# An FNet + SoLU kernel: three parts of the first transform turned later and by GpSimd, and the mean of the first four steps on ScalarE

## Chip, cores, metric

One core of one Trainium2 chip. The metric is the device time in microseconds (us), with the median of several executions. Profiles show one execution; times in them count from its start. "Faster" or "slower" needs 2%.

Names used throughout: PE is the matrix engine, DVE is VectorE, ACT is ScalarE, POOL is GpSimd, SP is SyncE. A "q" after the name of an engine is its sequencer. PEld is PE's loading of weights, which overlaps with its products (from 96 to 1140 us of the kernel before, PE is busy for all 1044 us and PEld for 797 of them).

## The reference

All is float32.

```python
x = randn(8, 3136, 256) * 0.1                       # batch, sequence, features
X = np.fft.fft(np.fft.fft(x, axis=1), axis=2).real  # FNet mixing
x = X.reshape(25088, 256)
h = x @ w_in                                        # 256 -> 1024
solu = h * softmax(h)
ln = (solu - mean) / sqrt(var + 1e-6) * g_ln
out = ln @ w_out                                    # 1024 -> 256
```

## The kernel before

The transform along the sequence (3136 = 49 x 64) is done in two stages. The result of the first stage goes to DRAM (`zd`). It is then read back with its axes changed, in five parts for each pair of batches: that is "turning" a part. Each part takes four requests of 160 KB:

```python
def turn(pr, i, engine=nc.gpsimd, a=0, b=KG):
    zd = pr.zd.rearrange("(k j) n d -> j n k d", j=4)
    ...
    for j in range(4):
        engine.dma_start(out=pr.g[i][j * NH : (j + 1) * NH, a:b, :], in_=zd[j, :, i * KG + a : i * KG + b, :])
```

The second stage and the expert layer then run in 100 steps, one `Unit` each. In each step PE computes `up` of the present unit, `transform2` for the unit two steps ahead, and `down` of the unit four steps back. A unit needs one row `r` of 512 bytes, spread by a DMA of its own (`spread`), before DVE can make `ev`. The operations that the change touches, and the loop:

```python
def spread(t):                                   # the tiny transfer "r"
    t.r = small.tile([P, 1], FP32, tag="r", name="r")
    nc.sync.dma_start(out=t.r, in_=t.q[0:1, P : 2 * P])

def product(t, s):                               # u = h * exp, with its sum; then -mean
    ...
    nc.vector.scalar_tensor_tensor(out=t.u[s], in0=t.h[s], scalar=1.0, in1=t.u[s], op0=ALU.mult,
                                   op1=ALU.mult, accum_out=t.usum[:, s : s + 1])
    nc.gpsimd.tensor_scalar(out=t.nmean[:, s : s + 1], in0=t.usum[:, s : s + 1], scalar1=-1.0 / FF,
                            scalar2=None, op0=ALU.mult)

def square(t, s):                                # (u - mean)^2, summed, on ScalarE
    ...

whole = 4                                        # these steps transpose u on PE, later ones by DVE and DMA
for i in range(len(units) + lag):                # lag = 4
    ...
        even(cur, up(cur, 0))                    # ev: waits for r
        ...
        ps_o = [down(old, s) for s in order]
        ...
        for s in cur.signs:
            product(cur, s)
        if i == 1:
            weights.centre()                     # wbar, then DVE centres the output weights
        for s in cur.signs:
            square(cur, s)
        ...
    if 0 < i + 1 < NK // KG:
        turn(first, i + 1, nc.sync)              # parts 1 to 4 in steps 0 to 3
    if ahd:
        ahead(ahd, cur.k1)                       # in step 0 it loads two blocks of the next pair
```

## Time and profile before

| | before | where it is read |
|---|---|---|
| time, median of 3 (range) | 1195.55 us (1193.29 to 1196.69) | the timed runs |
| span of the profiled run | 1191.5 us | page |
| PE busy | 97% | page, part 1 |
| first product of `down` starts | 96.16 us | timeline of PE |
| row r of step 3: requested, `ev` starts | 72.62, 85.52 us | chain of waits |
| last product of PE to the end of the span | 7.30 us | trace; the prediction did not look at it |

The kernel is bound by PE, which is full from 96 to 1140 us.

### The profile page before, as it was taken

What the parts mean: (1) busy time and instruction counts of PE and PEld (TensorE: products, weight loads), DVE (VectorE), ACT (ScalarE), POOL (GpSimd) and SP (SyncE); (2) the same over time, 40 slices, a digit from 0 to 9 for tenths busy, and PEclk for the clock granted to TensorE, in tenths of its full rate; (3) what the DMA queues carried; (4) which work ended last, traced back from release to release, by engine and by line L of the source; (5) the groups of instructions that cost most, each with busy time, mean ns of one, the idle gap of its engine ahead of it and who ended that gap; (6) DMA issues with size and microseconds to landing.
All of it is one profiled execution on the core that took longest, in us unless ns stands there. A gap on an engine that the chain in (4) does not pass through costs nothing.

```text
span 1191.5 us, 15914 instructions
## 1 busy us (share of the span) xinstructions
PE 1152.2 (97%) x4720; PEld 874.4 (73%) x4720; DVE 904.8 (76%) x1234; ACT 678.5 (57%) x1404; POOL 489.1 (41%) x950
## 2 busy tenths in 40 slices
PE   2979999999999999999999999999999999999997
PEld 1547777777777777778777777777777777777786
DVE  7889777777778877777768878777777887777770
ACT  4567565656546655555646656556565555565551
POOL 3034535434545444443544444442543333433342
PEclk9899999999999999999999999999999999999999
DMA  9693765756775765655775775663684444535433
GB/s 241 200 218 75 174 159 155 205 144 147 186 167 158 190 178 140 179 142 137 172 182 144 193 177 144 173 173 109 167 198 112 129 133 120 141 94 141 124 104 101
DMA packets 459797, 185.38 MB, mean 156 GB/s; under 512 B 425750, under 2 KB 442270, under 8 KB 459712
## 3 DMA queue, kind: packets, MB, share of 16 engines
q1 hardware_dynamic: 446720, 148.18, 49.3%
q0 software_dynamic: 12992, 36.19, 10.9%
q8 instruction: 38, 0.62, 0.2%
q14 instruction: 47, 0.39, 0.1%
HBM read 44.78 MB, written 38.80 MB: 70 GB/s over the span
## 4 chain that ended last, share of the span: by engine, by line
PE 93%; DMA 3%; DVE 1%; SPq 1%; issue 0%; ACT 0%; POOL 0%; DVEq 0%; ACTq 0%
PE ps_o L328 57%; PE ps_h L227 27%; PE ps L171 5%; PE ps L199 3%; DMA raw_in<-in_moe_w_in_dram 1%; DMA r<-q 1%; PE wps L459 1%; SPq L179 1%; DMA T<-in_t_tab_dram 0%; DVE y L123 0%; DVE xa L131 0%; DVE y L122 0%; ACT h L268 0%; SPq L364 0%; DVE ev L233 0%
## 5 line engine op out<-in xcount | busy, mean ns | idle before, releaser
L328 PE MATMUL ps_o<-Wo,uT 128*128 128x256 f32 x3136 | 693.2, 379 | 0.0
L328 PEld LDWEIGHTS ps_o<-Wo,uT 128*128 128x128 f32 x3136 | 611.0, 196 | 62.1 <-issue 0.9
L227 PE MATMUL ps_h<-Wi,q 128*128 128x512 f32 x800 | 361.6, 595 | 2.6 <-DVE ev L233 2.1
L259 DVE SCALAR_TENSOR_TENSOR u<-h,u 128x1024 f32<-128x1024 f32 x196 | 239.9, 1225 | 55.2 <-ACT u L251 28.8
L261 POOL TENSOR_SCALAR nmean<-usum 128x1 f32<-128x1 f32 x196 | 83.3, 425 | 455.2 <-DVE u L259 455.1
L241 DVE CUSTOM_DVE_ANT_0 h<-ev,ps_h 128x1024 f32<-128x1024 f32 x196 | 231.7, 1218 | 49.9 <-PE ps_h L227 38.6
L227 PEld LDWEIGHTS ps_h<-Wi,q 128*128 128x128 f32 x800 | 152.1, 191 | 152.2 <-issue 143.3
L268 ACT ACTIVATE h<-u,nmean 128x1024 f32<-128x1024 f32 x196 | 225.0, 1149 | 65.0 <-POOL nmean L261 64.0
L233 DVE SCALAR_TENSOR_TENSOR ev<-w_mid,r,ps_h 128x1024 f32<-128x1024 f32 x100 | 127.8, 1278 | 136.7 <-PE ps_h L227 122.5
L251 ACT ACTIVATE u<-h,neg 128x1024 f32<-128x1024 f32 x196 | 225.3, 1150 | 6.3
L296 DVE STREAM_TRANSPOSE v<-u 128x1024 f32<-128x1024 f32 x192 | 228.6, 1233 | 0.1
L205 ACT COPY q<-ps 128x256 f32<-128x256 f32 x100 | 37.0, 371 | 280.7 <-PE ps L199 245.2
L333 ACT ACTIVATE ot<-ps_o,rs 128x256 f32<-128x256 f32 x196 | 87.0, 461 | 60.2 <-PE ps_o L328 51.2
L340 POOL DMA_INDIRECT out_dram<-ot,idx x96 | 103.1, 1074 | 36.8 <-issue 20.9
L199 PEld LDWEIGHTS ps<-T,g 128*128 128x128 f32 x400 | 60.1, 191 | 48.3 <-issue 45.8
L171 PE MATMUL ps<-y,F 98*100 98x258 f32 (+3 forms) x288 | 71.4, 385 | 23.7 <-DVE y L124 23.7
L283 POOL TENSOR_TENSOR rs<-v,neg_half 128x2 f32<-128x2 f32 (+1 forms) x100 | 84.1, 841 | 7.8
L249 ACT ACTIVATE neg<-nmax 128x1 f32<-128x1 f32 x196 | 38.2, 195 | 64.8 <-DVE nmax L241 64.8
L171 PEld LDWEIGHTS ps<-y,F 98*100 98x100 f32 x288 | 45.6, 177 | 35.6 <-DVE y L124 21.6
L280 POOL TENSOR_SCALAR v<-ssq 128x2 f32<-128x2 f32 (+1 forms) x100 | 23.1, 231 | 113.9 <-ACT h L268 113.9
L199 PE MATMUL ps<-T,g 128*128 128x128 f32 x400 | 60.7, 275 | 0.6 <-DMA g<-zd 0.6
L131 POOL TENSOR_TENSOR xa<-xa,xb 98x1020 f32<-98x1020 f32 (+1 forms) x24 | 54.5, 2272 | 0.0
(72 smaller groups left out, 441.9 us busy)
## 6 DMA issues: line engine op xcount, KB each, us to landing
uT<-v SPq DMA_DIRECT2D x752, 128.0 KB
out_dram<-ot SPq DMA_DIRECT2D x100, 128.0 KB
xa<-in_x_dram SPq DMA_DIRECT2D x28, 392.0 KB
zd<-z SPq DMA_DIRECT2D x24, 400.0 KB
g<-zd POOLq DMA_DIRECT2D x60, 160.0 KB, 4.7
g<-zd SPq DMA_DIRECT2D x16, 160.0 KB
raw_in<-in_moe_w_in_dram SPq DMA_DIRECT2D x4, 512.0 KB
raw_out<-in_moe_w_out_dram SPq DMA_DIRECT2D x2, 1024.0 KB
```

Of the source, the lines that this page charges most:

```text
L171: nc.tensor.matmul(o[..., cs], F[:, 2 * t + h, :], i[..., cs], start=first, stop=True, skip_group_check=True)
L199: nc.tensor.matmul(o, g[:, k, h * P : (h + 1) * P], table, start=(h == 0), stop=True, skip_group_check=True)
L227: nc.tensor.matmul(ps[:, fs], t.q[:, c * P : (c + 1) * P], Wi[:, c, fs], start=True, stop=True)
L233: nc.vector.scalar_tensor_tensor(out=t.ev, in0=w_mid, scalar=t.r, in1=ps, op0=ALU.mult, op1=ALU.add)
L241: nc.vector.tensor_tensor_reduce(out=t.h[s], in0=t.ev, in1=ps, scale=1.0, scalar=-3.0e38, op0=ALU.subtract if s else ALU.add, op1=ALU.max, ...
L251: nc.scalar.activation(out=t.u[s], in_=t.h[s], func=ACT.Exp, bias=t.neg[:, s : s + 1], accum_out=t.esum[:, s : s + 1])
L259: nc.vector.scalar_tensor_tensor(out=t.u[s], in0=t.h[s], scalar=1.0, in1=t.u[s], op0=ALU.mult, op1=ALU.mult, accum_out=t.usum[:, s : s + 1])
L268: nc.scalar.activation(out=t.h[s], in_=t.u[s], func=ACT.Square, bias=t.nmean[:, s : s + 1], accum_out=t.ssq[:, s : s + 1])
L296: nc.vector.transpose(out=t.batch.v[:, t.w, :, o], in_=t.u[s])
L328: nc.tensor.matmul(ps, uT[:, c, :, s], Wo[:, c, :], start=(c == 0), stop=(c == KF - 1))
L333: nc.scalar.mul(out=t.ot[s], in_=ps, mul=t.rs[:, s : s + 1])
L340: dma = nc.gpsimd.indirect_dma_start(out=out, out_offset=bass.IndirectOffsetOnAxis(ap=idx[:, i : i + 1], axis=0), in_=t.ot[s], in_offset=None)
```

## The change

Two intentions. The 1.92 MB of parts 2 to 4 leave the crowded start, where SyncE's queue also carries the rows `r`, and are requested by GpSimd in steps 5, 8 and 11, shortly before they are used. And in the first four steps, the mean is made on ScalarE, so that the square, also on ScalarE, need not wait for GpSimd.

```diff
-    def product(t, s):
+    def product(t, s, alone):
...
-        nc.gpsimd.tensor_scalar(out=t.nmean[:, s : s + 1], in0=t.usum[:, s : s + 1], scalar1=-1.0 / FF,
-                                scalar2=None, op0=ALU.mult)
+        if alone:
+            nc.scalar.mul(out=t.nmean[:, s : s + 1], in_=t.usum[:, s : s + 1], mul=-1.0 / FF)
+        else:
+            nc.gpsimd.tensor_scalar(...)                      # as before
...
-                    product(cur, s)
+                    product(cur, s, i < whole)
...
-            if 0 < i + 1 < NK // KG:
-                turn(first, i + 1, nc.sync)
+            if i == 0:
+                turn(first, 1, nc.sync)
+            elif i in (5, 8, 11):
+                turn(first, (i + 1) // 3)                     # by GpSimd
```

More of the change, by code (lines that the diff above doesn't have):

```diff
@@ L260, in product @@
                                        op1=ALU.mult, accum_out=t.usum[:, s : s + 1])
-        nc.gpsimd.tensor_scalar(out=t.nmean[:, s : s + 1], in0=t.usum[:, s : s + 1], scalar1=-1.0 / FF,
-                                scalar2=None, op0=ALU.mult)
+        if alone:
+            nc.scalar.mul(out=t.nmean[:, s : s + 1], in_=t.usum[:, s : s + 1], mul=-1.0 / FF)
+        else:
+            nc.gpsimd.tensor_scalar(out=t.nmean[:, s : s + 1], in0=t.usum[:, s : s + 1], scalar1=-1.0 / FF,
+                                    scalar2=None, op0=ALU.mult)
     def square(t, s):
```

## The prediction

> **What bounds the kernel now.** I read the page first (busy times, slices, chain), then a table of windows, then the chain of the start alone, then the timelines of each engine between 58 and 130 us. Page, parts 1 and 2:
>
> ```profile
> PE 1152.2 (97%) x4720; PEld 874.4 (73%) x4720; DVE 904.8 (76%) x1234; ACT 678.5 (57%) x1404; POOL 489.1 (41%) x950
> ...
> PE   2979999999999999999999999999999999999997
> ```
>
> PE is full in every slice but those at the start and the very end. The windows (length, then busy us of PE, PEld, DVE, ACT, POOL) put the border at 96 us:
>
> ```profile
> 0.00:96.00 96.00, 63.99 (x235) 38.80 (x236) 77.06 (x138) 52.66 (x95) 25.37 (x47) 0.93 0.83 212
> 96.00:1140.00 1044.00, 1044.00 (x4291) 797.38 (x4290) 812.76 (x1077) 610.31 (x1279) 446.78 (x876) 1.00 0.59 153
> ```
>
> From 96 to 1140 us PE has no gap at all. So the change can shorten the kernel only by making that full stretch begin earlier, and lengthen it only by delaying that begin or tearing a gap into it. The first product of the down projection starts at 96.16 us. What sets that is in the chain of waits between 66 and 97 us (start, length, what):
>
> ```profile
> 66.73 5.83 DMA T<-in_t_tab_dram
> ...
> 72.62 12.80 DMA r<-q
> ...
> 85.52 1.29 DVE ev L233
> ...
> 91.77 1.15 POOL nmean L261
> ...
> 92.94 0.23 ACT h L268
> ...
> 95.32 0.26 ACT q L205
> 95.63 0.66 PE ps_t L308 x4
> ```
>
> One tiny transfer, the row r of the unit of step 3 (512 bytes, "r3" from here), holds 12.8 of these 30 us. It was requested at 72.62 and landed at 85.42. After it comes a serial chain of VectorE and ScalarE work, 10.1 us, to the last transposes of that step. The chain crosses both things that the change touches: the mean (GpSimd) and the queue in which the parts are turned (SyncE). The SyncE queue, in order:
>
> ```profile
> 65.46 2.45 SPq L445 DMA_DIRECT2D T<-in_t_tab_dram  x2
> ...
> 69.55 1.79 SPq L187 DMA_DIRECT2D g<-zd  x4
> 71.39 0.86 SPq L109 DMA_DIRECT2D xa<-in_x_dram  x2
> 72.62 0.51 SPq L210 DMA_DIRECT2D r<-q  x1
> 73.56 4.50 SPq L187 DMA_DIRECT2D g<-zd  x4
> 80.29 0.48 SPq L210 DMA_DIRECT2D r<-q  x1
> 82.47 4.25 SPq L187 DMA_DIRECT2D g<-zd  x4
> ```
>
> The reader is to see that r3 stands *ahead* of the third part (73.56) and behind the second part (69.55) and two loads of the next pair (71.39). The change takes out the groups at 73.56, 82.47 and the later one at 87.34, all behind r3. It leaves everything ahead of r3.
>
> [...] What stands behind r3 in the same queue should then not hold it up. The trace agrees. In its packet records the 196 packets of 4096 bytes of the two loads start between 76.5 and 83.7 us on the hardware queue, and r3 lands 1.4 us after the last of them. [...] from 79.5 to 81.5 us 12 to 15 packets of the loads and about 2 of the next part (1024 bytes) are open at a time. [...]
>
> **The mean, part by part.** Step 3 in the timeline of all engines:
>
> ```profile
> 85.52 1.28 DVE L233 SCALAR_TENSOR_TENSOR ev<-w_mid,r,ps_h 128x1024 f32<-128x1024 f32 x1 [4.26 <-DMA r<-q]
> ...
> 89.62 0.19 ACT L249 ACTIVATE neg<-nmax 128x1 f32<-128x1 f32 x1
> ...
> 91.60 1.22 DVE L259 SCALAR_TENSOR_TENSOR u<-h,u 128x1024 f32<-128x1024 f32 x1
> 91.77 1.35 POOL L261 TENSOR_SCALAR nmean<-usum 128x1 f32<-128x1 f32 x2 [6.63 <-DVE u L259]
> ...
> 92.94 1.15 ACT L268 ACTIVATE h<-u,nmean 128x1024 f32<-128x1024 f32 x1 [1.86 <-POOL nmean L261]
> ```
>
> The first of the two means starts at 91.77 and its row of the trace is 1.14 us long, against 0.23 for one that runs free. It sits behind the second product (91.60 to 92.82)[...]. The square starts at 92.94, 0.12 us after the second product ends. So ScalarE waits 1.86 us for a mean whose own work is 0.2 us. That looks like a gain of about 1 us, but not in the order in which the code issues: the loop makes product and mean of both signs first, then both squares. On ScalarE[...] the queue is then mean 0, mean 1, square 0, square 1. Mean 1 needs the second product, which ends at 92.82. It starts about 0.06 us later and holds ScalarE about 0.23 us (the small negation of the same shape: 0.19 long, next one 0.23 after its start). Square 0 can start at about 93.11 in place of 92.94: 0.17 us *later*. [...] On the path that adds +0.17 us in step 3. The same happens in step 2, and in step 0, which has one sign, the mean gains about 0.1 us; neither is on the path, as r3 comes later than both. In step 1 the scaling of wbar on ScalarE (0.36 us) now falls behind two means, and VectorE's centring of the output weights starts some 0.75 us later, at 72.5. VectorE idles 4.26 us before r3 lands, so this is swallowed too.
>
> **The parts turned later.** Removed from the early SyncE queue: 3 x 4 requests, 1.92 MB. Effect on r3's request: none, it waits for the table T (landed 72.55), because a request waits for the one eight earlier in that queue and T is eight before r3 in both kernels. Effect on r3's landing: the third part ran[...] until about 82 us, then beside the last 23 or so packets of the loads. Those that started at 82.1 to 82.7 took 500 to 640 ns against 290 to 370 just before. If the third part's traffic caused that, two packets in a row on the slowest engine could each save 0.25 us; if not, nothing. I take -0.2 us on the path. The next row (requested 80.29) goes out some 4.5 us earlier, but its user was not waiting for it. Added later: 4 requests on GpSimd at the end of steps 5, 8 and 11. The trace has such groups already, for the later pairs:
>
> ```profile
> 300.01 2.37 POOL L187 DMA_DIRECT2D g<-zd  x4
> ```
>
> 2.4 us each in a step of 11.65 us, in which GpSimd at that stage is busy about half (5 us in 12), and before its next mean it had 2.9 us of idle in the steps 4 and 5. A mean that comes late by a few tenths delays ScalarE, which is not the bound and feeds a product four steps on. The third part, requested near 113 us, must have landed when step 8 takes it, near 137 us; such groups landed in 4.6 us in the middle. PE stayed full through the stretches in which the later pairs do this. Cost: 0.
>
> **Sum.** +0.17 - 0.2 + 0 = about 0 us. Predicted: 1195.4 us.
>
> **Rivals.** (A) The third part does hold r3 up[...]. Then r3 would land before VectorE is through with step 2 (about 82 us), and the start would move by up to 85.5 - 82.0 = 3.5 us: 1192 us. For it: r3 takes 12.8 us, DMA share is at 1.0 throughout. Against: [...]the loads that end just before it, and that about 1.42 MB of the second part and the loads, plus the gathered rows of the GpSimd queue (0.78 MB), stand ahead and alone fill most of that time at 190 GB/s (2.2 MB: 11.6 us). (B) [...] the squares of step 3 start 1 us earlier, 1194.4 us. Against: the issue order above. (C) GpSimd's added requests in steps 5 to 11 push means and load gathers so far that PE runs dry: each gap of PE would add 1 to 3 us, 1197 to 1201 us. Against: later pairs. (D) Without the turned parts around 84 to 92 us nothing changes in PE's clock, which dips to half at 88 us[...]; it comes back by itself and those matmuls are not on the chain.
>
> **Range and chances.** The three runs before span 3.4 us by themselves, more than any of my terms. With rival A or B on one side and C on the other: 1191.5 to 1198.0 us. A change of 2% is 24 us; the whole idle time of PE between 60 and 96 us is only 7.8 us, so faster by over 2% is all but excluded (0.01), slower would need many gaps in the full stretch (0.01), the same 0.98.
>
> **What would show it.** Right: the chain of the start still has r3 landing near 85 us, the square of step 3 starts 0.25 to 0.3 us after the second product with the mean of the second sign on ScalarE ahead of it, the first down product at 96 us within 0.5, and PE at 100% from there to 1140. Wrong: r3 landing at 84 us or sooner (A), a square that starts right after the first product (B), or gaps of PE after 110 us with waits that lead back to GpSimd (C).

## The result, and the profile after

| | before | after |
|---|---|---|
| median of 4 runs (range), same chip | 1195.66 us (1193.29 to 1196.69) | 1190.70 us (1188.54 to 1191.48) |
| ratio of means, 95% interval | | 0.9958 (0.9939 to 0.9978) |

Ratios here and below are the mean time of one kernel's fast runs over that of the other's of the same rounds, so not quite the ratio of the medians quoted. The kernel became about 5 us shorter; the prediction said 1195.4 and its range began at 1191.5, so the result lies just outside. Where I speak of a gain below, I mean that its interval excludes 1.

First, the part that held. Windows of the changed kernel (length, then busy us of PE, PEld, DVE, ACT and POOL with counts, PE clock, DMA share, GB/s):

```profile
0.00:96.00 96.00, 65.65 (x239) 39.78 (x240) 77.96 (x140) 54.60 (x104) 23.50 (x40) 1.00 0.72 191
...
96.00:1140.00 1044.00, 1044.00 (x4284) 797.17 (x4283) 811.78 (x1074) 609.46 (x1276) 452.58 (x887) 1.00 0.61 154
```

PE is full from 96 to 1140 us again, although GpSimd now requests three parts inside this stretch. From the sixth step to the last, the products of `up` in the two traces keep a constant distance, 0.65 us. So nothing was won or lost between these, and the 5 us must be at the ends.

**The start.** SyncE's queue of the changed kernel (start, length of issuing, request, count):

```profile
66.65 2.35 SPq L448 DMA_DIRECT2D T<-in_t_tab_dram  x2
...
72.76 0.85 SPq L109 DMA_DIRECT2D xa<-in_x_dram  x2
74.49 20.55 SPq L210 DMA_DIRECT2D r<-q  x4
```

After the loads there are only the rows `r`; the three groups of `g<-zd` are gone. This trace reached that place later: it requests the table T at 66.65 us, 1.19 us after the trace of before (65.46). The first product of `up` was already 1.04 us later (57.21 against 56.17), and no instruction ahead of it was changed, so I count this as scatter (in the second trace of the same kernel, r_after below, T is requested at 65.43 us) and measure the start from the request of T on. In both traces the request of the row waits for T, the request eight before it in SyncE's queue (0.3 us before, 0.8 us after, put down to T in SyncE's waits). The chain of waits of the changed kernel (start, length, what):

```profile
74.49 9.88 DMA r<-q
...
84.47 1.29 DVE ev L233
...
91.82 0.20 ACT nmean L262
...
94.59 0.66 PE ps_t L311 x4
95.25 5.29 PE ps_o L331 x16
```

The row took 9.88 us where it took 12.80. From the request of T to `ev` of step 3 it is 84.47 - 66.65 = 17.82 us, before 85.52 - 65.46 = 20.06: 2.24 us less. From `ev` to the first product of `down` it is 10.65 us against 10.64 before, so the mean on ScalarE changed nothing. The reason is in the timeline of ScalarE:

```profile
91.82 0.20 ACT L262 ACTIVATE nmean<-usum 128x1 f32<-128x1 f32 x1 [0.94 <-DVE u L259]
91.93 1.13 ACT L271 ACTIVATE h<-u,nmean 128x1024 f32<-128x1024 f32 x1
```

ScalarE waits 0.94 us for the second product of DVE, makes the second mean, and only then the first square. The square starts 0.16 us after that product ends (91.77); it was 0.12 us before.

The last line of the chain is a surprise. The first 16 products of `down` take 5.29 us on it; in the trace of before the group of 16 was 3.73 long. The window shows why (same columns as above, changed kernel):

```profile
95.00:99.00 4.00, 4.00 (x13) 3.16 (x12) 3.65 (x7) 3.68 (x9) 0.88 (x2) 0.57 0.02 0
```

The clock granted to PE is 0.57 in this stretch. In the clock records it is at one half from 95.4 to 98.8 us. The clock records of the two traces hold no other share than one half and 1.00, and inside the kernel a stretch at half lasts 3.41 us (this one, and one in before's trace at 87.2 to 90.6 us, where PE had slack) or 10.24 us (before's trace, from 25.8 us on). Here it fell on the path. I put its cost at about 1.7 us, the 5.29 against the 3.60 us that the same 16 products take on before's chain, at a clock of 1.00, and the 3.61 on those of loads_late and all_three. A second run of the same changed kernel (below) has the dip at 84.6 to 88.0 us, off the path.

**The end.** This I had not looked at before predicting. GpSimd ends with three DRAIN instructions; the one that starts first is the longest. In the view of one source line (shortest/median/longest in ns, first and last start), first the kernel before:

```profile
L734 POOLq DRAIN  x3: 46/102/9363, 1181.4 to 1191.2; - x3
```

then the changed one:

```profile
L739 POOLq DRAIN  x3: 46/102/3323, 1182.3 to 1188.7; - x3
```

Before, GpSimd drains for 9.36 us from 1181.4, so until 1190.7 us. PE ended at 1184.2 and the last DMA packet started at 1186.1 us: nothing else that the trace shows is still running, and the core ends at 1191.5. That the DRAIN is what holds it is a reading here; experiment 6 tests it. After, it takes 3.32 us and the output transfer sets the end. What SyncE waits for in the last 8 us shows the same (who waits, for whom, us in total, times, longest), before:

```profile
SPq L734 <- PEq L734: 4.7, 2, 4.2
```

and after:

```profile
SPq L739 <- PEq L739: 0.7, 2, 0.5
```

The wait is put down to PE's sequencer, but PE had been done for long. I read it as a barrier of all engines at the end, to which GpSimd comes last: in before's view of that source line GpSimd's semaphore instructions start at 1190.8 us, 0.1 us after its DRAIN ends, and those of ACT, DVE and PE at 1190.9. From PE's last product to the end it is 7.30 us before and 3.82 after.

So this one trace says -2.2 (row) + 1.7 (clock, by chance) - 3.5 (end) = -4.0, plus a start that is about 1.1 us later by scatter; the spans differ by 2.6 us. The rest, 0.25 us, PE loses among its last products (see experiment 6). Two gains, one of which I had in the sum at a tenth of its size and the other not at all, had to be taken apart on the chip.

### The profile page after: what moved, and what is told of

Its sections match the earlier page's. It is cut to its first block, busy times and chain, and to the rows that moved or that the text cites. A ratio compares the mean times of both kernels' runs of the same rounds, so it can differ in the third digit from the quotient of the medians.

```text
span 1188.9 us, 15920 instructions
## 1 busy us (share of the span) xinstructions
PE 1154.8 (97%) x4720; PEld 875.7 (74%) x4720; DVE 905.3 (76%) x1234; ACT 679.6 (57%) x1411; POOL 493.0 (41%) x955
## 4 chain that ended last, share of the span: by engine, by line
PE 94%; DMA 2%; DVE 2%; ACT 1%; issue 1%; SPq 0%; DVEq 0%; ACTq 0%
PE ps_o L331 57%; PE ps_h L227 28%; PE ps L171 5%; PE ps L199 3%; DMA raw_in<-in_moe_w_in_dram 1%; PE wps L462 1%; DMA r<-q 1%; DVE u L259 0%; ACT h L271 0%; DVE y L123 0%; DVE h L241 0%; ACT u L251 0%; DVE xa L131 0%; DVE y L122 0%; SPq L367 0%
## 5 line engine op out<-in xcount | busy, mean ns | idle before, releaser
L264 POOL TENSOR_SCALAR nmean<-usum 128x1 f32<-128x1 f32 x189 | 76.6, 405 | 428.7 <-DVE u L259 428.3
L187 POOL DMA_DIRECT2D g<-zd x76 | 45.4, 610 | 30.1 <-DMA zd<-z_g 26.8
```

## The experiments

Theories at the outset. R: the transfers standing *behind* the row slow it. M: the mean gives something. E: the end shortens because GpSimd makes more requests. Rivals to R: it is the queue (SyncE's own, and the order in it) and not the traffic, or it is only the reading of DRAM. For each run I give "start": from the request of T to the first product of `down`, "end": from PE's last product to the end, and the length of GpSimd's longest DRAIN. In the text steps count from 0; some of the expectations count them from 1 (steps 6, 9 and 12 for 5, 8 and 11).

| run | median us (runs) | ratio (95%) | start | end | GpSimd requests, DRAIN us |
|---|---|---|---|---|---|
| before (first profile) | 1195.66 (4) | | 30.70 | 7.30 | 200, 9.36 |
| after (first profile) | 1190.70 (4) | 0.9958 (0.9939 to 0.9978) | 28.47 | 3.82 | 212, 3.32 |
| r_after | 1188.71 (5) | 0.9951 (0.9937 to 0.9964) | 28.60 | 3.55 | 212, 3.32 |
| turns_only | 1188.24 (5) | 0.9947 (0.9933 to 0.9961) | 28.48 | 3.55 | 212, 3.32 |
| mean_only | 1194.04 (5) | 1.0002 (0.9988 to 1.0015) | 31.26 | 7.30 | 200, 9.36 |
| turns_early_pool | 1192.55 (5) | 0.9982 (0.9969 to 0.9996) | 33.31 | 3.55 | 212, 3.32 |
| turns_late_sync | 1192.63 (6) | 0.9991 (0.9976 to 1.0006) | 27.61 | 7.31 | 200, 9.36 |
| loads_late | 1186.09 (6) | 0.9932 (0.9917 to 0.9947) | 25.99 | 3.56 | 212, 3.32 |
| mean_between | 1187.59 (6) | 0.9948 (0.9933 to 0.9963) | 27.42 | 3.77 | 212, 3.32 |
| all_three | 1187.18 (6) | 0.9948 (0.9931 to 0.9966) | 27.39 | 3.77 | 212, 3.32 |
| loads_pool_12 | 1191.04 (6) | 0.9961 (0.9947 to 0.9976) | 30.61 | 3.55 | 212, 3.24 |
| loads_pool_8 | 1193.85 (1) | | 31.44 | 3.30 | 208, 3.16 |
| loads_pool_4 | 1191.22 (1) | | 30.79 | 3.53 | 204, 3.03 |
| loads_pool_2 | 1196.02 (1) | | 31.98 | 7.38 | 202, 9.45 |
| loads_pool_16 | 1191.61 (1) | | 30.77 | 3.31 | 216, 3.32 |
| extra_dram | 1191.80 (4) | 0.9978 (0.9963 to 0.9993) | 31.19 | 3.31 | 212, 3.33 |
| extra_sbuf | 1190.68 (4) | 0.9975 (0.9960 to 0.9990) | 30.87 | 3.30 | 212, 3.32 |
| loads_late_between | 1184.81 (5) | 0.9920 (0.9906 to 0.9934) | 25.60 | 3.56 | 212, 3.32 |

The medians of the kernel before in the four groups of runs were 1194.76, 1193.67, 1194.78 and 1194.70 us. The column "start" also shows the scatter: the seven traces with the old queue and the old loads at the start (before, mean_only and the five loads_pool) lie between 30.6 and 32.0 us, the three with the changed queue (after, r_after, turns_only) between 28.5 and 28.6. The two groups don't overlap; their means, 31.1 and 28.5, are 2.6 us apart. Three ratios lie just outside the ranges that were expected, beside those told below: turns_late_sync (0.997 to 0.999), mean_between (0.9935 to 0.9945) and loads_pool_12 (0.9965 to 0.9975).

**1. The change again (r_after).** No edit.

> The changed kernel again, for a second trace and more rounds. All theories: ratio to the kernel before 0.994 to 0.998 (1188.5 to 1193 us). Queue theory (the parts behind r3 share the DMA engines' time with the loads ahead of it, so taking them away lets r3 land about 2.2 us sooner): r3 lands 17.5 to 18.2 us after the request of the table T, against 20.0 in the kernel before. Chance theory (the gain of the profiled run came from the tail after the last matmul, 6.7 us before and 3.2 us after): the tail differs from the first trace by over 1 us.

1188.71 us against 1194.76 for the kernel before on the same chip, 6.05 us less. The row and the end come out as in the first profile, and the dip of the clock does not lie on the path. The two terms are (28.60 - 30.70) + (3.55 - 7.30) = -5.85 us, but the span of this trace is only 4.93 us shorter than before's (1186.59 against 1191.52). The difference is just before the end: from the last group of `up` to PE's last product this trace needs 0.96 us more, as PE waits once for ScalarE to empty an output buffer:

```profile
1168.98 14.06 PE L331 MATMUL ps_o<-Wo,uT 128*128 128x256 f32 x64 [0.70 <-ACT ot L336]
```

Experiment 6 comes back to it. With the clock off the path, this trace still gives the cleaner account.

**2. One half of the change each (turns_only, mean_only).**

```diff
 # turns_only: the changed kernel with
-                    product(cur, s, i < whole)
+                    product(cur, s, False)
 # mean_only: the kernel before with the hunks of product() alone
```

> The turned parts moved to steps 6, 9 and 12, the mean left on GpSimd. Queue theory: the whole gain, and 0.1 to 0.2 us more since the mean on ScalarE costs 0.17: 1190 to 1191 us, ratio within 0.001 of the changed kernel's. Mean theory (the gain is that of the mean): ratio 0.999 to 1.001, 1195 to 1196 us.

> The mean on ScalarE in the first four steps, the parts turned as before. Queue theory: no gain, ratio 1.000 to 1.001, the square of step 3 starts 0.28 us after the end of the second product (0.12 before). Mean theory: ratio 0.995 to 0.998.

The turns alone give the whole gain (0.9947), the mean alone gives none (1.0002), and the interval of mean_only leaves no room for more than 2 us either way. Theory M falls. The chain of turns_only:

```profile
72.56 10.21 DMA r<-q
...
82.88 1.29 DVE ev L233
...
89.13 1.15 POOL nmean L264
```

The mean is back on GpSimd, with its 1.15 us behind the product, and the start (28.48 us) is no longer for it.

**3. When, or by whom (turns_early_pool, turns_late_sync).** The two parts of moving the turns, each alone.

```diff
 # turns_early_pool: the kernel before with
-            if 0 < i + 1 < NK // KG:
-                turn(first, i + 1, nc.sync)
+            if i == 0:
+                turn(first, 1, nc.sync)
+            elif i + 1 < NK // KG:
+                turn(first, i + 1, nc.gpsimd)
 # turns_late_sync: the changed kernel with
-                turn(first, (i + 1) // 3)
+                turn(first, (i + 1) // 3, nc.sync)
```

> As before, but the third to fifth part requested by GpSimd in steps 2 to 4 and not by SyncE: the traffic stays where it was, only the queue is another. If what counts is traffic beside the loads and r3: no gain or a loss (ratio 0.999 to 1.004), with r3 landing 20 us or more after the request of T. If what counts is only that SyncE's queue holds the later rows up: the gain of the changed kernel, 0.994 to 0.998.

> The changed kernel, but the three late parts requested by SyncE: GpSimd makes 200 requests as in the kernel before, not 212. Two-gains theory (2.2 us at the start from the traffic, 3.75 us at the end because the number of GpSimd's requests sets how long its last drain takes): r3 lands 17.5 to 18.2 us after T's request, but the end takes 7.3 us after the last matmul as in the kernel before; ratio 0.997 to 0.999. If the short end comes from the early parts being out of SyncE's queue: end 3.5 us, ratio 0.994 to 0.996.

They separate the two gains neatly. Late on SyncE: the start is short (27.61 us), the end stays long (7.31), and GpSimd has its 200 requests. Early by GpSimd: the start is long, the end short. Early by GpSimd is even worse for the row than the kernel before: `ev` of step 3 comes 22.67 us after the request of T, against 20.06. In GpSimd's queue the third part does not stand behind the row, it runs beside the loads and the row: packets of GpSimd's queue start until 90.8 us, the last of the loads at 85.1. What helps the start is therefore the *time*, not the other engine. (Its ratio, 0.9982, is a little below the range that I had given, because the short end was not in that expectation.) The time of turns_late_sync gained less than its start promised (0.9991): in its trace the half clock lay at 93.7 to 97.1 us, on the first products of `down` (5.29 us for 16), as in the first profile of the changed kernel. Whether this holds for its other five runs is not shown.

**4. What stands ahead of the row (loads_late).** The two loads of the next pair go from step 0 to step 3.

```diff
 # turns_only with, in ahead():
-        if step == 0:
+        if step == (3 if pr.p == 1 else 0):
             load(pr, 0)
             load(pr, 1)
```

> The variant with the parts moved and the mean left on GpSimd, and the loads of the second pair requested in step 3 rather than step 0, so that they stand behind r3. If the loads ahead of r3 are what holds it: r3 lands before VectorE is through with step 2, the wait of 1.6 us and more at ev is gone, the first down product starts 1.4 to 3 us sooner, ratio 0.992 to 0.994. If something else holds r3 (its own 128 small pieces, the table T): no change from 0.9947.

1186.09 us, 0.9932; with turns_only at 0.9947 the intervals overlap, but the start is another 2.5 us shorter and the chain has another shape:

```profile
65.76 5.18 DMA zd<-z_g
...
72.43 4.32 DMA g<-zd
...
81.75 1.15 POOL nmean L264
```

The row of step 3 is no longer in it. The chain now crosses the second part itself, and the transfer that writes what it reads. So the loads do hold the row up. The edit takes away their place ahead of the row and their traffic at once, so it does not tell these two apart. Traffic behind matters in addition.

**5. The mean that does pay, and its price (mean_between, all_three).** Each square directly behind its mean, in the loop of the products, so that ScalarE does not queue the second mean before the first square; then this with the late loads.

```diff
 # mean_between: the changed kernel with
                 for s in cur.signs:
                     product(cur, s, i < whole)
+                    if i < whole:
+                        square(cur, s)
...
                 for s in cur.signs:
-                    square(cur, s)
                     if i >= whole:
+                        square(cur, s)
                         turn_blocks(cur, s)
 # all_three: this and the edit of loads_late
```

> The changed kernel with each square right behind its mean in the first four steps (product 0, mean 0, square 0, product 1, mean 1, square 1). Order theory (the mean on ScalarE gains nothing because mean 1 stands ahead of square 0): square 0 of step 3 starts about 0.3 us after the first product instead of the second, the first down product 0.9 to 1.2 us sooner, ratio 0.9935 to 0.9945. Rival (square 0 is not on the path): no change, 0.995.

> The changed kernel with the loads in step 3 and each square behind its mean. Both theories right: r3 is no wait any more and the squares start earlier in every step, so the gains add or more: first down product 3 to 5 us sooner than in the changed kernel, ratio 0.990 to 0.993. If one of them is wrong: 0.993 to 0.995.

In the trace of mean_between, `ev` to `down` falls from 10.65 to 9.90 us, and the start from 28.5 to 27.42. The times don't show it (0.9948 beside 0.9947 for turns_only in another group, with intervals of 0.0014 to each side), so the gain is unclear. all_three did not add up (0.9948, where I had hoped for 0.990 to 0.993), and its chain tells why:

```profile
73.25 0.28 ACT wbar L493
...
75.76 1.29 DVE ev L233
...
77.09 5.40 PE ps_h L227 x8
```

In step 1, the scaling of `wbar` on ScalarE now stands behind both means and both squares. DVE centres the output weights later and makes `ev` of the next step later, and PE waits 1.92 us for that; then the eight products of `up` take 5.40 us in place of 3.4 to 3.7. My prediction had called this delay of `wbar` swallowed. That holds while the row is late; with the row early it is the path. The chain of mean_between already runs this way (`wbar` at 72.91, `ev` at 75.42, `up` 5.40 us), which fits that the late loads add nothing to its start: 27.42 and 27.39 us.

**6. The end by itself (loads_pool_12, then 8, 4, 2 and 16).** A change without anything to do with the start: N of the plain loads of the later pairs are requested by GpSimd in place of SyncE.

```diff
 # the kernel before with, in load():
-        nc.sync.dma_start(out=xa, in_=x_pn[r, c * CH + 1 : (c + 1) * CH + 1, :])
+        engine = nc.gpsimd if 0 <= (pr.p - 2) * NC + c < 12 else nc.sync
+        engine.dma_start(out=xa, in_=x_pn[r, c * CH + 1 : (c + 1) * CH + 1, :])
```

> The kernel before, but 12 of the direct loads of the third and fourth pair (near 400 and 650 us, where PE is full and nothing waits) are requested by GpSimd, so that it makes 212 requests as in the changed kernel. Nothing in the first 100 us differs. Count theory (the number of GpSimd's requests sets the length of its last drain): drain 3.3 us and 3.5 us from the last matmul to the end, ratio 0.9965 to 0.9975. If the short end belongs to the turned parts only: drain 9.36 us, ratio 1.000.

> As above with 8 loads, 208 requests, one look: if the drain goes by the number of requests in steps, its length here is either 3.3 or 9.36 us; a value between would mean that it grows with each.

> As above with 4 loads, 204 requests, one look: drain 9.36 us if the border is above 204, 3.3 us if below.

> As above with 2 loads, 202 requests, one look: drain 9.36 us if the border is above 202, 3.3 us if below; a length other than these two would fell the theory of two lengths.

> The kernel before with 16 loads requested by GpSimd, 216 requests, one look. A single border near 203 requests: drain 3.3 to 3.4 us, end 3.3 to 3.6 us after the last matmul. A repeating border: 9.4 us possible.

With 12 loads moved, the start is that of before (30.61), the end is short (3.55), and the time falls to 0.9961: 4.7 us by the ratio, with an interval of 2.9 to 6.3, which holds the 3.75.

```profile
L735 POOLq DRAIN  x3: 46/97/3240, 1182.6 to 1188.7; - x3
```

Theory E is upheld, and it does not matter that these transfers are others than those of the change. (Requests are what I counted; whether it is their number or the number of pieces that they are cut into is not told apart.) The others look for where it turns. Four requests more (204 in all):

```profile
L735 POOLq DRAIN  x3: 46/97/3030, 1183.9 to 1189.0; - x3
```

and two more (202):

```profile
L735 POOLq DRAIN  x3: 46/97/9445, 1183.5 to 1193.4; - x3
```

Between 202 and 204 requests the longest DRAIN goes from 9.45 to 3.03 us. At 208, 212 and 216 it is short as well. So it is not a matter of the change's 12, and not of late requests (those of the change are out by 185 us, the DRAIN comes a millisecond later). What GpSimd does in those 6 us the trace does not show, but it shows a counterpart. Where there are 204 requests or more, GpSimd also pauses before one of its last requests, the 203rd to the 208th, with nothing that the trace shows to wait for. In r_after:

```profile
1155.97 2.47 POOL L325 DMA_DIRECT2D uT<-v  x4 [2.62 <-DVE v L299]
1160.51 2.31 POOL L325 DMA_DIRECT2D uT<-v  x4 [2.07 <-issue]
```

The kernel before makes these eight requests in one go:

```profile
1158.10 4.76 POOL L322 DMA_DIRECT2D uT<-v  x8 [2.62 <-DVE v L296]
```

In 13 of the 14 traces with 204 requests or more this pause, among these eight requests or right after them, is 1.6 to 2.3 us (in loads_pool_4 it comes later and is mixed with a wait for data); in the four traces with 200 or 202 there is none at this place. It delays the requests that store the last outputs, and so the buffers that ScalarE and PE wait for. Part of the gain is thus paid back: from the last group of `up` to PE's last product, these 14 traces need 0.0 to 1.1 us more than before's (r_after 0.96, loads_pool_12 1.08). The span of loads_pool_12 is 2.5 us shorter than before's: -3.75 at the end, +1.08 ahead of it, +0.2 at the start.

**7. Is it the traffic, and which side of it (extra_dram, extra_sbuf).** Both are turns_only with the third part's place in the early queue filled again. In extra_dram it is turned early as before, and once more in step 5. In extra_sbuf the early transfer has the same size and the same pieces of 1 KB, but reads from a weight that lies on chip. The results stay right, as the true part overwrites it.

```diff
 # extra_dram: turns_only with
+            elif i == 1:
+                turn(first, 2, nc.sync)
 # extra_sbuf: turns_only with
+            elif i == 1:
+                first.g[2] = gpool.tile([P, KG, D], FP32, tag="g", name="g")
+                for j in range(4):
+                    nc.sync.dma_start(out=first.g[2][j * NH : (j + 1) * NH], in_=<256-wide pieces of Wi>)
 # both: the turn in step 5 writes the same buffer again
```

> The variant with the parts late and the mean on GpSimd, plus the third part turned early as well, in step 2 by SyncE right behind r3, only for its traffic (it is turned again in step 6; the result stays right). Traffic theory: this alone brings the late landing back, r3 19.5 to 20.5 us after T's request (17.8 without it), the packets of 4096 bytes of the loads 310 to 350 ns on average (251 without it); ratio 0.9965 to 0.998. If it is the fourth and fifth part, or the later rows: 17.5 to 18.2 us and 0.9945.

> The same number of requests, pieces and bytes in the same place, but read from on-chip memory (the input weights) and not from DRAM, into the same buffer. If reading DRAM is where the parts and the loads collide: r3 lands as without extra traffic, 17.5 to 18.2 us after T's request, loads' packets 240 to 265 ns. If it is the DMA engines or the writing side: as with the DRAM source, 19.5 us or more and 310 ns or more.

The start is long again in both, 31.19 and 30.87 us; in extra_dram `ev` of step 3 comes 20.56 us after the request of T, against 17.83 in turns_only. The queue of extra_sbuf has the filler right behind the row:

```profile
73.17 0.52 SPq L211 DMA_DIRECT2D r<-q  x1
74.03 6.45 SPq L667 DMA_DIRECT2D g<-Wi  x4
```

and its chain the row:

```profile
73.17 12.56 DMA r<-q
```

It takes 12.56 us, as before the change. So 640 KB behind the row are enough, and it does not matter that they no longer come from DRAM: the theory that the reading of DRAM is what is shared falls. Left are the DMA engines and the writing side, which these runs don't tell apart. Both kernels keep the short end and so stay a little shorter than the kernel before (0.9978, 0.9975).

That the filler slows what stands *ahead* of it is in the packet records. The 196 packets of 4096 bytes of the two loads take on average 347 ns before, 332 in mean_only, 358 in extra_dram, 334 in extra_sbuf, but 257 in after, 249 in r_after and 251 in turns_only. Counted from the request of T, the last of them starts after 18.26 us before and after 16.79 in turns_only. So 1.5 us of the row's 2.2 are the loads in front of it, the rest is the row itself. The windows of 82 to 84 us show how the crowd differs (DMA share and GB/s are the last two columns), before:

```profile
82.00:84.00 2.00, 0.38 (x4) 0.14 (x2) 0.00 (x0) 2.00 (x6) 0.27 (x2) 1.00 0.94 120
```

and after:

```profile
82.00:84.00 2.00, 1.66 (x15) 1.30 (x13) 0.88 (x2) 1.08 (x2) 0.93 (x1) 1.00 0.32 68
```

Before, the 16 DMA engines are 94% busy while only 120 GB/s move; DVE has no work at all, as it waits for the row. After, they are 32% busy and DVE works (0.88 of the 2 us).

**8. The best of all (loads_late_between).** all_three, with mean and square paired on ScalarE in steps 2 and 3 only, so that `wbar` in step 1 keeps its place.

```diff
 # all_three with
-                    product(cur, s, i < whole)
-                    if i < whole:
+                    product(cur, s, i in (2, 3))
+                    if i in (2, 3):
                         square(cur, s)
...
-                    if i >= whole:
+                    if i not in (2, 3):
                         square(cur, s)
+                    if i >= whole:
                         turn_blocks(cur, s)
```

> For the best version: parts late on GpSimd, loads of the second pair in step 3, and the mean on ScalarE with its square right behind it, but in steps 3 and 4 only, since in step 2 it delays the scaling of wbar and the centring behind it. If the failure of all three changes together comes from that delay in step 2: first down product 1 to 2 us sooner than with the loads moved alone, ratio 0.9915 to 0.993. If not: 0.993 to 0.995.

```profile
70.05 4.22 DMA g<-zd
...
80.39 1.20 DVE ev L233
...
86.50 0.21 ACT nmean L262
...
86.74 1.24 ACT h L271 x2
```

1184.81 us, ratio 0.9920 (0.9906 to 0.9934). It beats the kernel before and the changed one (0.9951), and the intervals don't meet; against loads_late alone (0.9932) they overlap. The expectation of a start 1 to 2 us shorter than with the late loads alone was missed: it is 0.4 us shorter. The first mean and its square start before the second product is done, `wbar` is not in the chain, and the start is 25.60 us.

## Why the prediction was wrong

The prediction followed the right place, the row of step 3, and the right terms of the start, but missed by 4.7 us (6.7 against r_after), for two reasons that the runs keep apart.

**"From 96 to 1140 us PE has no gap at all. So the change can shorten the kernel only by making that full stretch begin earlier": the step that failed first.** The first sentence is right. The conclusion leaves out what comes after the last product. There GpSimd's DRAIN held the kernel for 3.75 us, and twelve more requests on GpSimd, counted as "Cost: 0", took it away (up to 1.1 us of it is paid back just before). loads_pool_12 shows this gain alone; turns_late_sync shows its absence. It was in the trace of before, 7.30 us from PE's last product to the end, but nothing there would have told me that more requests shorten it.

**"I take -0.2 us on the path" for the third part's effect on the row: mis-sized.** It measured -2.2 us in the pair of profiles (2.6 between the groups of traces). I took it that what stands behind the row in its queue does not hold it up; this was an assumption, and not shown by any trace. What stands ahead does: the row lands after the loads in front of it (in the kernel before, 1.4 us after the end of their last packet), and when these move (loads_late) it is off the chain. But I took the third part to run beside the loads at no cost to them, and charged only the last packets at 82.1 to 82.7 us. From 79.25 to 82 us one to three of its packets are open at a time, beside 11 to 16 of the loads, and the loads' packets are slower while it runs, 347 ns on average in place of about 250. The clue stood there: I put slower packets down to a few at the end because I compared them with "290 to 370 just before", which were slowed already, though packets that started at 81.3 to 81.4 us in the same trace took 244 to 262. Rival A had the size (up to 3.5 us, 1192 us); I rejected it on that assumption and on the sum of bytes at 190 GB/s, and that rate (the window from 72 to 84 us) was itself a rate with the third part in it.

**The mean: right in kind, +0.17 us predicted, about 0 measured.** The order mean, mean, square, square is in the trace as foretold (they start at 90.67, 91.82, 91.93 and 93.06 us). The square starts 0.16 us after the second product where I expected 0.25 to 0.3, since ScalarE starts the next instruction 0.11 us after the start of the small one, not 0.23 (in loads_late_between, where the square reads the mean just before it, it is 0.24). Rival B did not come about. With the square moved behind its mean it does, in the trace.

**`wbar` behind two means, "swallowed": right** in the changed kernel. Counted from the request of T, the centring starts 0.4 us later in r_after (71.75 and 72.12 us), where 0.75 was foretold. It holds as long as the row is later; mean_between and all_three show the limit.

**The late turns at no cost: right.** PE has no gap, and rival C did not come about. Such a group in the changed kernel, in the timeline of GpSimd:

```profile
146.50 2.46 POOL L187 DMA_DIRECT2D g<-zd  x4
```

**The clock dip "not on the chain" (rival D): half right.** It lies on the path in some executions (+1.7 us in the first profile of the changed kernel) and not in others, in kernels with the same start, so it is scatter and no property of the change.

A small slip in its readings: the loads' packets start at 76.3 us, not 76.5.

What stays open: what the DRAIN does in its 6 us, why its length turns between 202 and 204 requests, and what GpSimd pauses for where it is short; and whether the loads are slowed in the DMA engines or at the writing side.

## What to carry to other kernels

Here a small transfer that a whole chain waits for was delayed not only by what stood ahead of it in its queue, but also by what was requested right behind it (2.7 us at `ev`, extra_dram against turns_only): look for bulk traffic within some microseconds on both sides and move it to a time when nobody waits for a row. Always read the end of the kernel as well, from the last useful instruction to the end of the span, and ask what ends last there (here GpSimd's longest DRAIN, 9.36 us before and 3.32 after). And where two means stood between two products and two squares, moving them to the engine of the squares gained nothing in that order; with the order changed the trace shows 0.75 us, the times do not.
